# Another hand-written order from the third chunk on, and the rows of maxima loaded one pair a portion

## The chip, the cores and the metric

The kernel runs on one core of a Trainium2 chip. A core has TensorE (PE in the profile; its weight loads are listed as PEld), VectorE (DVE), ScalarE (ACT), GpSimd (POOL) and SyncE (SP, which here only issues DMA transfers). Each engine takes its instructions strictly in the order in which the program lists them, and waits where an operand or a buffer is not ready. The metric is the device time of one execution in microseconds, as the median of several runs.

## The reference

Linear attention over 8 batches, 8 heads, 576 positions and head width 64, then a gated feed-forward over all 4608 tokens:

```python
q_s = softmax(q, over the head width);  k_s = softmax(k, over the positions)
kv  = einsum('bhsd,bhse->bhde', k_s, v)
x   = einsum('bhsd,bhde->bhse', q_s, kv)      # -> 4608 tokens x 512
a, b = x @ w_a, x @ w_b                       # 512 x 1536 each
out = (a * b) @ w_out                         # 1536 x 512
```

All in float32. The kernel gets its precision by splitting an operand into a high and a low part (tiles xo, ws, gh/gl, qhl) and adding three products: high by high, high by low, low by high.

## The kernel before

**Chunks, pairs, portions.** The 4608 tokens are worked on in nine chunks (0 to 8) of 512. Chunk 0 runs beside the loading and conversion of the weights. From chunk 1 on a chunk is six *pairs* of feed-forward blocks (loop at L1392). One pair makes seven products instead of eight (a Strassen-Winograd step on 2 x 2 blocks): A11 into kx, S2 into ky, S3 into ka, S1 into kp, A12 onto kx, S4 onto kp, A22 onto ka (L1434 to L1471). Each is twelve matmuls with 256 columns. kx, ky, ka and kp are banks of PSUM, and there are few: ky and kp share one, and a second product into kx, kp or ka may start only when DVE or ACT has read the first (L1437, L1455, L1441), as the next pair's first product may only when the last has been read (L1457, L1468, L1473). Beside the seven products a pair holds the output projections of the pair before (`run_pending`, matmuls into po with 512 columns, L867), and three calls of `attend` (L1425, L1450, L1465).

**Attention of the next chunk.** While chunk c is multiplied, the attention for chunk c + 1 is computed in *portions*, one at each call of `attend` (class Spread), 15 in a chunk. `attention_tasks` builds the list of portions. For a chunk from the fourth (index 3) on it holds: portions 0 to 4, the maxima and sums of q's softmax (L675 to L683), which are transposed on PE (pst, L689), copied (sst, L691) and written to DRAM as dq (L693); portions 0 to 5, the keys of the next batch: loads (L503, L509), the maximum over the positions (L524 to L526 on DVE, L515 on POOL), exponential (L547, L550), and the product with v (pk, L585); then the *rows*: for each of four head pairs g, dq's rows of maxima and of sums are loaded back and spread over 64 partitions each (`q_rows`, four transfers "mr<-dq", L719), together with a transposed block of q ("qtt<-in_q_late", L707); at last, for each g, the row of maxima is added to that block (L725), ACT takes the exponential (L726), the result is split (L343, L346), multiplied with kv (px, L764) and scaled by the row of sums (xf, L963). For chunks 4 to 8 the row loads of group g stood in portion 6 + g and its use in portion 10 + g and 11 + g; for chunk 3 two groups share a portion.

**Weights.** From chunk 2 on the seven weight operands of a pair come from DRAM, 512 KB each ("ws<-dw", L478), into eight buffers; those of a chunk's last pair are held for the next chunk's first. All loads and stores are issued on SP's queue. A load waits there until the product eight operands before it has been made, and everything behind it on the queue waits too.

**The order.** The text `ORDER` (L28) lists for each engine the instructions of the first chunks one by one. An item is `name:place*count`: of the instructions traced under that name and not yet listed, take the one at this place (0 if not written), count times. `pair.k`, `proj.k`, `attend.k`, `early.k`, `late.k` and `wj.k` are the products and their DVE and ACT work, the projections, the portions, the operands made from x for the next chunk, and the load of weight operand j, of pair k, counted from chunk 1's first; so pair.6 to pair.11 are chunk 2. `arrange` (L1305) chains the instructions of an engine in that order. What the list does not name comes behind it, in the order that the compiler's planner finds by simulating the program: from what is ready, first what was traced first. Before, the list ends on PE within pair.10, on SP with a weight load for pair.11; chunks 3 to 8 are the planner's.

Of the kernel before, what the change touches and what calls it, by code (L numbers as in the profile page):

```python
# [213 lines left out]
    ),  # L214
    "Pool": (
# [4 lines left out]
    ),  # L220
# [37 lines left out]
def linear_attention_then_gated_ffn(  # L258
# [18 lines left out]
    nc = tc.nc  # L277
# [15 lines left out]
    NI = w_ab.shape[0]  # L293
# [97 lines left out]
    def load_f(f):  # L391
# [7 lines left out]
        with tc.issue_after(ins.ins):  # L399
            nc.sync.dma_start(out=raw, in_=w_out[f])  # L400
# [520 lines left out]
    def attention_tasks(c):  # L921
# [48 lines left out]
        for i in range(max(len(stats), len(steps))):  # L970
            seq.append((stats[i] if i < len(stats) else []) + (steps[i] if i < len(steps) else []))
# [560 lines left out]
```

## Time and profile before

| | us |
|---|---|
| median of 3 runs | 945.16 (944.64 to 946.18) |
| the profiled execution | 942.09 |
| its span, first to last instruction | 940.3 |
| mean granted clock of TensorE | 0.998 |

A row of the timeline gives the start and the duration in us, the engine, the line, the operation, the tile written and those read, and the count of like instructions merged into the row; the bracket at its end gives the idle time of that engine just before, and what ended it. SPq is SP's queue. In a row of the windows the columns are the stretch, its length, the busy time and count of PE, PEld, DVE, ACT and POOL, the granted clock of TensorE (1.00 is full speed), the mean busy share of the DMA engines and GB/s. Matmuls overlap and their ends are modelled, so waits of PE are best seen from start to start.

### The profile page before, as it was taken

The numbers are of one execution on the slowest core, as the hardware profiler recorded it, in microseconds if no ns is written. First come the engines' busy times: TensorE is split into PE (matmuls) and PEld (weight loads), VectorE is DVE, ScalarE is ACT, GpSimd is POOL, SyncE is SP. The second block draws the span as 40 slices with busy tenths as digits, with TensorE's granted clock in tenths as the row PEclk, the third lists the DMA queues.
The fourth block names the chain that finished last, engine by engine and source line by source line (L and its number), as shares of the span: only waits on it lengthen the run. The fifth ranks groups of instructions, "written<-read, shape, count | busy, mean of one in ns | idle before, by whom it ended". The sixth has DMA issues, their size and how long they took to land.

```text
span 940.3 us, 17539 instructions
## 1 busy us (share of the span) xinstructions
PE 925.3 (98%) x6565; PEld 837.1 (89%) x6565; DVE 615.2 (65%) x1218; ACT 394.2 (42%) x1094; POOL 107.8 (11%) x88
## 2 busy tenths in 40 slices
PE   8999999999999999999999999999999999999998
PEld 6777789999889899999999999999999998999997
DVE  7998898778655677467656574666657454744433
ACT  8988775435522245133613271324424351322111
POOL 2555434420000000000100010000000000000000
PEclk9999999999999999999999999999999999999999
DMA  9989899989779879983999288945996388637761
GB/s 355 362 293 374 326 327 337 325 295 309 261 252 293 260 262 352 336 281 111 345 268 353 90 302 280 374 167 188 331 343 226 102 292 304 204 108 263 252 218 51
DMA packets 88947, 253.27 MB, mean 269 GB/s; under 512 B 10720, under 2 KB 11296, under 8 KB 88864
## 3 DMA queue, kind: packets, MB, share of 16 engines
q1 hardware_dynamic: 88864, 252.16, 76.5%
q8 instruction: 52, 0.85, 0.4%
q14 instruction: 31, 0.25, 0.1%
HBM read 213.09 MB, written 36.93 MB: 266 GB/s over the span
## 4 chain that ended last, share of the span: by engine, by line
PE 93%; DMA 2%; DVE 2%; SPq 1%; ACT 1%; issue 0%; POOL 0%; DVEq 0%
PE po L867 30%; PE ka L838 14%; PE kp L838 14%; PE kx L838 14%; PE pt L808 7%; PE ky L838 7%; PE px L764 2%; PE pk L585 2%; DMA ws<-dw 2%; PE po L853 1%; SPq L719 1%; PE px L752 1%; DMA kt_first<-in_kt 0%; DVE mc L1122 0%; PE pq L739 0%
## 5 line engine op out<-in xcount | busy, mean ns | idle before, releaser
L867 PE MATMUL po<-wo_w,gh 128*128 128x512 f32 x840 | 264.4, 396 | 0.0
L838 PE MATMUL ka<-xo,ws 128*128 128x256 f32 x1152 | 181.5, 283 | 2.7 <-DVE u L1441 1.9
L838 PE MATMUL kx<-xo,ws 128*128 128x256 f32 x1152 | 183.9, 282 | 0.0
L838 PE MATMUL kp<-xo,ws 128*128 128x256 f32 x1152 | 176.0, 283 | 0.0
L867 PEld LDWEIGHTS po<-wo_w,gh 128*128 128x128 f32 x840 | 151.6, 189 | 25.3 <-issue 0.4
L838 PEld LDWEIGHTS ka<-xo,ws 128*128 128x128 f32 x1152 | 160.1, 190 | 8.8 <-issue 3.2
L838 PEld LDWEIGHTS kx<-xo,ws 128*128 128x128 f32 x1152 | 160.5, 189 | 4.9
L838 PEld LDWEIGHTS kp<-xo,ws 128*128 128x128 f32 x1152 | 156.9, 189 | 5.3 <-DVE cc L1455 0.2
L867 PE MATMUL po<-wo_w,gl 128*128 128x512 f32 x420 | 153.7, 396 | 0.0
L343 ACT CAST gh<-cc 128x512 fp32r<-128x512 f32 x96 | 58.0, 620 | 146.8 <-DVE cc L1469 131.8
L1456 ACT COPY cc<-kx 128x256 f32<-128x256 f32 x48 | 17.9, 372 | 179.9 <-PE kx L838 174.9
L867 PEld LDWEIGHTS po<-wo_w,gl 128*128 128x128 f32 x420 | 78.1, 188 | 15.2 <-DVE gl L346 0.4
L838 PE MATMUL ky<-xo,ws 128*128 128x256 f32 x576 | 86.8, 281 | 2.2 <-DMA ws<-dw 1.1
L1468 DVE TENSOR_TENSOR cc<-kp,u 128x512 f32<-128x512 f32 x48 | 33.1, 690 | 85.1 <-PE kp L838 84.7
L808 PE MATMUL pt<-xo,ws 128*128 128x512 f32 x288 | 87.1, 418 | 0.0
L678 ACT ACTIVATE qt<-qt,st 128x64 f32<-128x64 f32 x224 | 75.4, 340 | 18.4 <-DVE st L675 15.6
L838 PEld LDWEIGHTS ky<-xo,ws 128*128 128x128 f32 x576 | 76.9, 189 | 3.9 <-DVE qtt L725 1.3
L346 DVE TENSOR_TENSOR gl<-cc,gh 128x512 fp32r<-128x512 f32 x96 | 67.0, 706 | 15.0 <-ACT gh L343 12.3
L1455 DVE TENSOR_TENSOR cc<-kp,u 128x512 f32<-128x512 f32 x48 | 33.1, 691 | 66.6 <-PE kp L838 66.2
L808 PEld LDWEIGHTS pt<-xo,ws 128*128 128x128 f32 x288 | 53.0, 188 | 17.4 <-issue 4.3
L515 POOL PARTITION_ALL_REDUCE mx<-m x20 | 17.7, 895 | 438.8 <-DVE m L526 419.1
L1437 ACT COPY u<-kx 128x512 f32<-128x512 f32 x48 | 28.0, 583 | 63.1 <-PE kx L838 55.6
(150 smaller groups left out, 1116.9 us busy)
## 6 DMA issues: line engine op xcount, KB each, us to landing
ws<-dw SPq DMA_DIRECT2D x260, 512.0 KB, 5.5
dw<-ws SPq DMA_DIRECT2D x42, 512.0 KB, 6.4
mr<-dq SPq DMA_DIRECT2D x112, 128.0 KB, 4.5
raw<-in_w_ab SPq DMA_DIRECT2D x24, 512.0 KB, 7.2
out<-ot SPq DMA_DIRECT2D x36, 256.0 KB, 5.0
vt<-in_v SPq DMA_DIRECT2D x28, 325.0 KB, 6.8
qt<-in_q SPq DMA_DIRECT2D x32, 256.0 KB, 5.2
kt<-in_k SPq DMA_DIRECT2D x24, 320.0 KB, 4.9
```

The costliest lines, as they stand in the source:

```text
L343: nc.scalar.copy(out=hi, in_=src)
L346: return nc.vector.tensor_tensor(out=lo, in0=src, in1=hi.bitcast(F32), op=ALU.subtract)
L585: nc.tensor.matmul(pk[h * D:(h + 1) * D], kt[:, j, h], vt[:, j, h], start=(j == 0), stop=(j == J - 1),)
L678: nc.scalar.activation(out=qt[:, j, h], in_=qt[:, j, h], func=AF.Exp, bias=st[:, h, 0, j:j + 1], accum_out=st[:, h, 1, j:j + 1],)
L764: nc.tensor.matmul(px[:, s], w, m[:, s], start=(i == 0), stop=(i == 2))
L808: nc.tensor.matmul(pt, w[:, wp], x[g][:, xp], start=(g == 0 and i == 0), stop=(g == NP - 1 and i == 2),)
L838: ins = nc.tensor.matmul(pt[:, n], w[:, n, wp, c], x[:, xp, c], start=(first and n == 0 and i == 0), stop=(i == 5), skip_group_check=True,)
L867: ins = nc.tensor.matmul(po[t], a[:, ts], wo[f][:, w], start=(f == ends[0] and i == 0), stop=(f == ends[1] and i == 2),)
L1437: nc.scalar.copy(out=u2, in_=kx)
L1455: nc.vector.tensor_tensor(out=cc[:, 3], in0=kp, in1=u3, op=ALU.add)
L1456: nc.scalar.copy(out=cc[:, 0, 0], in_=kx[:, 0])
L1468: nc.vector.tensor_tensor(out=cc[:, 1], in0=kp, in1=u2, op=ALU.add)
```

## The change

Three edits. The kernel's arithmetic, its tiles and its transfers stay the same in kind and number.

1. In `ORDER`, the lists of all five engines are replaced from a point in chunk 2's first pair on (on PE, from the entry after "pair.6:23*3 proj.6 proj.6:1"). Up to that point they stay as they were. The new PE list ends seven matmuls into pair.11, the one of SP with w5.11, the first load of chunk 4's attention and the first store of chunk 1.
2. `load_f` drops the `issue_after` that put the load of w_out behind that of w_ab. SP's list, which names these loads one by one, is unchanged there.
3. `attention_tasks`, for chunks 4 to 8: portions 6 and 7 are left empty; the rows of group g and its block of q are in portion 8 + g; their use stays in portions 10 to 14.

The diff, with most of the list left out:

```diff
     "PE": (
...
-        "pair.6 proj.6:2 pair.6:24 proj.6:7 pair.6 proj.6:3 pair.6:23*3 proj.6 proj.6:1 pair.6*4 "
...
-        "attend.10*3 pair.10 attend.10 "
+        "pair.6 proj.6:2 pair.6:24 proj.6:7 pair.6 proj.6:3 pair.6:23*3 proj.6 proj.6:1 pair.6*8 "
...
+        "attend.10 pair.11*5 pair.10 attend.10 pair.11 attend.10 pair.11 "
     "DVE": (
...
-        "early.5 pair.5 attend.6 attend.6:3 late.5 attend.6:1 attend.6:2 late.5 pair.6 pair.6:1 "
-        "attend.6:2 pair.6 attend.6:2 attend.7:3 attend.7 attend.6:1 pair.6:1 pair.6*2 pair.6:1*2 "
-        "pair.7 attend.6:1 attend.6:2*3 pair.6*2 attend.7:5 pair.7 attend.7:5 pair.7 attend.6 "
-        "pair.7:1 attend.6:1 attend.7:7 attend.7 attend.7:6*2 attend.7:1 attend.7*2 attend.7:1 "
-        "attend.6*2 pair.7 attend.7:2 attend.7:1 attend.6 attend.7 pair.7*2 pair.7:1 pair.7 "
...
-        "pair.9:1 pair.9*2 attend.9 attend.9:1 pair.9 attend.9 pair.10*2 early.11 attend.9 pair.10 "
-        "attend.9*2 pair.10:1 pair.10*2 "
+        "early.5 attend.6 attend.6:3 attend.6:1 pair.5 attend.6:1 pair.6 late.5*2 pair.6 attend.6:4 "
+        "attend.6:1*2 pair.6 attend.6:1 attend.7:3 attend.6 pair.6:1 pair.6 attend.7 pair.6 "
+        "pair.6:1*2 attend.7:5 pair.6 pair.7 attend.6*5 pair.6 pair.7 attend.7:5*2 attend.7:6*2 "
+        "attend.7:2 pair.7 pair.7:1 attend.7*2 attend.6 attend.7 pair.7 attend.7:2 attend.7:1*2 "
+        "attend.7 pair.7:3 attend.6 pair.7*3 attend.7 pair.7 attend.7*3 pair.8*2 attend.7 attend.8 "
...
+        "pair.9 attend.9 pair.9:1 pair.9*6 attend.9 pair.10 attend.7 pair.10 attend.9:1 attend.9 "
+        "pair.9 pair.10 attend.9 pair.10 attend.9:1 attend.9 pair.10:1*2 early.11:1 pair.10 "
     "Activation": (
...
-        "attend.6:4 attend.6:3 attend.6 pair.6 late.5 attend.6:1 attend.7 attend.6 attend.7:5 "
-        "attend.7:7 proj.6:1 attend.7:7 attend.7:6 attend.7:2 proj.6:2 attend.7:6 attend.7:2 pair.7 "
-        "attend.7:7 pair.6 attend.7:6 attend.7:5 proj.6 attend.7 attend.7:2 proj.6 pair.6 attend.7:2 "
-        "pair.7 attend.7*2 attend.7:1 attend.7 pair.7 pair.8 pair.7 attend.8*2 pair.8*2 attend.9 "
...
+        "attend.6:4 attend.6:3 attend.6 late.5 pair.6 attend.6 proj.6:1 attend.6 proj.6:2 attend.7:6 "
+        "pair.6 proj.6*2 pair.7 attend.7:11 attend.7:3 attend.7:10 attend.7:11 attend.7:7 attend.7:6 "
+        "attend.7:5 pair.6 attend.7:3 attend.7:1 attend.7 attend.7:1 pair.7 attend.7:2 attend.7:1*2 "
+        "attend.7*2 pair.8 attend.7 pair.7*2 attend.8 pair.8 attend.8 pair.8 pair.9 attend.9*2 pair.8 "
...
     "Pool": (
...
-        "sums.0*8 sums.1*4 sums.2*4 sums.4 sums.3*2 sums.4 sums.3*2 sums.4*2 attend.6:1 attend.6 "
-        "attend.7*2 "
+        "sums.0*8 sums.1*4 sums.2*4 sums.4 sums.3*2 sums.4 sums.3*2 sums.4*2 attend.6*2 attend.7:1 "
+        "attend.7 "
     "SP": (
...
-        "attend.7 attend.6:2 w2.7 w1.7 proj.0 attend.6*2 w4.7 w3.7 w5.7 attend.7 w6.7 attend.7:1 w0.8 "
-        "attend.7*2 w2.8 w1.8 w4.8 attend.7 w3.8 w6.8 attend.8:8 w5.8 attend.8 attend.8:1 w0.9 w1.9 "
...
+        "attend.7 attend.6:2 attend.6 w1.7 attend.6 w2.7 proj.0 w4.7 attend.7 w3.7 w0.8 attend.7:1 "
+        "w6.7 w5.7 w2.8 attend.7:1 attend.7 w1.8 attend.8:8 w4.8 attend.7 attend.8:8 w3.8 w6.8 "
...
+        "attend.8 w3.11 attend.8 w6.11 w5.11 attend.12 proj.6 "
...
@@ load_f
-        with tc.issue_after(ins.ins):
-            nc.sync.dma_start(out=raw, in_=w_out[f])
+        nc.sync.dma_start(out=raw, in_=w_out[f])
...
@@ attention_tasks
+        last = pipeline(last)
+        if c > 3:
+            begin = 3 * NI - 3 - len(last) - 2
+            seq += [[] for _ in range(len(seq), begin)]
+            for g in range(NP):
+                seq[begin + g:begin + g + 1] = [rows[g:g + 1] + turned[g:g + 1]]
+            for n, now in enumerate(last):
+                seq[begin + n + 2:begin + n + 3] = [(seq[begin + n + 2] if n + 2 < NP else []) + now]
+            return seq
         if roomy(c):
 
             step = 2 if c < 4 else 1
             seq += [rows[g:g + step] + turned[g:g + step] for g in range(0, NP, step)]
-        return seq + pipeline(last)
+        return seq + last
```

`pipeline` staggers the steps of the four groups, so that `last` has five entries for four groups; with NI = 6 that makes begin = 8.

77 rows, old and new, of the table ORDER are left out of this document.

## The prediction

> **What bounds the kernel now.** I read the page first, then the timeline of PE, then the windows (for the granted clock), then the timelines of the engines that PE waited for.
>
> ```profile
> span 940.3 us, 17539 instructions
> ...
> PE 925.3 (98%) x6565; PEld 837.1 (89%) x6565; DVE 615.2 (65%) x1218; ACT 394.2 (42%) x1094; POOL 107.8 (11%) x88
> ...
> PE 93%; DMA 2%; DVE 2%; SPq 1%; ACT 1%; issue 0%; POOL 0%; DVEq 0%
> ```
>
> TensorE holds 93% of the chain that ended last, and the change neither adds nor removes a matmul. So the time can only move by what PE waits and by the clock it gets. The timeline of PE, from the first changed entry of its list (counted along the trace, that is at 239.2 us) to the end, has these starts after an idle time; the bracket gives it and what ended it:
>
> ```profile
> 242.77 0.28 PE L838 MATMUL kp<-xo,ws 128*128 128x256 f32 x1
> 244.98 0.36 PE L838 MATMUL ka<-xo,ws 128*128 128x256 f32 x1 [1.93 <-DVE u L1441]
> ...
> 266.76 0.27 PE L689 MATMUL pst<-ident,st 128*64 128x128 f32 x1 [0.90 <-DVE st L683]
> ...
> 270.47 0.45 PE L585 MATMUL pk<-vt,kt 128*64 128x65 f32 x7 [0.84 <-ACT kt L550]
> ...
> 322.29 0.33 PE L764 MATMUL px<-qhl,kvh 128*128 128x192 f32 x1 [1.19 <-DVE xf L963]
> ...
> 491.50 0.48 PE L838 MATMUL ka<-xo,ws 128*128 128x256 f32 x2 [0.77 <-DMA ws<-dw]
> ...
> 588.75 0.99 PE L838 MATMUL kx<-xo,ws 128*128 128x256 f32 x7
> 590.81 0.35 PE L838 MATMUL ky<-xo,ws 128*128 128x256 f32 x1 [1.07 <-DVE gl L346]
> ...
> 789.05 0.60 PE L838 MATMUL ky<-xo,ws 128*128 128x256 f32 x3 [1.12 <-DMA ws<-dw]
> ```
>
> They add up to 7.82 us. Between them matmuls follow each other evenly: seven in 0.99 us, so (0.99 - 0.28) / 6 = 0.12 us each for 256 columns. The first wait costs more than itself, as the windows show (the column after POOL is the granted clock):
>
> ```profile
> 246.50:247.00 0.50, 0.50 (x4) 0.50 (x4) 0.50 (x1) 0.00 (x0) 0.44 (x1) 0.50 1.03 406
> 247.00:249.00 2.00, 2.00 (x10) 1.90 (x10) 2.00 (x4) 1.15 (x3) 0.00 (x0) 0.50 0.85 284
> ...
> 246.00:250.00 4.00, 4.00 (x19) 3.64 (x18) 3.23 (x5) 1.91 (x5) 0.94 (x2) 0.57 0.86 311
> 320.00:324.00 4.00, 2.81 (x23) 2.60 (x22) 3.05 (x6) 0.78 (x2) 0.00 (x0) 1.00 0.56 185
> ```
>
> From 246 to 250 us the clock was 0.57, which costs 4 x 0.43 = 1.7 us; around the 1.19 us wait at 322 it stayed 1.00. So 7.82 + 1.7 = 9.5 us is all there is to gain, 1% of the time.
>
> **The change, part by part.** *The joined list, chunk 2 (239 to about 325 us).* The list fixes each engine's order there, so I followed what each waiting matmul needs through the old rows and the new order.
>
> Wait at 245. The second product into ka (L1471) overwrites the sums that L1441 reads, and L1441 was late on DVE:
>
> ```profile
> 242.62 0.37 ACT L1456 COPY cc<-kx 128x256 f32<-128x256 f32 x1 [3.77 <-PE kx L838]
> 242.89 0.62 ACT L343 CAST xo<-xt 128x512 fp32r<-128x512 f32 x1
> ...
> 238.53 0.68 DVE L1438 TENSOR_TENSOR u<-ky,u 128x512 f32<-128x512 f32 x1
> ...
> 243.54 0.69 DVE L346 TENSOR_TENSOR xo<-xt,xo 128x512 fp32r<-128x512 f32 x1 [1.72 <-ACT xo L343]
> 244.15 0.68 DVE L1441 TENSOR_TENSOR u<-ka,u 128x512 f32<-128x512 f32 x1
> ...
> 245.08 0.28 DVE L526 TENSOR_TENSOR m<-m,kt 128x128 f32<-128x128 f32 x1
> ...
> 246.26 1.05 DVE L547 TENSOR_TENSOR kt<-kt,mx 128x640 f32<-128x640 f32 x1
> ```
>
> DVE stood 1.72 us for the cast of `late.5`, which ACT held behind the copy of kx. The new lists put that cast before the copy ("late.5 pair.6" for "pair.6 late.5") and L1441 before the two late differences ("pair.6 late.5*2"). What is late next: ahead of L1441 the list now has the first L547, which needs GpSimd's reduction. L1438 starts at 238.53; then one 128x512 difference, the small L682, L524 and L526 bring L526 to about 240.1; from L526 to L547 it was 246.26 - 245.08 = 1.18, so L547 at 241.3, L1441 about 1.0 later, at 242.3, and PE goes on 244.98 - 244.15 = 0.83 after that, 243.1. PE comes to this matmul as the 26th entry instead of the 28th, at about 242.7: 0.4 us are left, and 0.1 where L1455, now behind the two differences, frees kp. A wait so short should not lower the clock. Gain 1.93 + 1.7 - 0.5 = **3.1** (bounds 0 and 3.6).
>
> Waits at 267 and 270:
>
> ```profile
> 263.94 0.28 PE L838 MATMUL kx<-xo,ws 128*128 128x256 f32 x1
> ...
> 264.26 0.38 ACT L1456 COPY cc<-kx 128x256 f32<-128x256 f32 x1 [5.18 <-PE kx L838]
> ...
> 264.87 0.34 ACT L678 ACTIVATE qt<-qt,st 128x64 f32<-128x64 f32 x1
> ...
> 265.33 0.17 DVE L682 TENSOR_SCALAR st<-st 128x8 f32<-128x8 f32 x1 [1.43 <-ACT qt L678]
> ...
> 266.67 1.39 POOL L515 PARTITION_ALL_REDUCE mx<-m  x2 [19.73 <-DVE st L683]
> ...
> 268.09 1.56 DVE L547 TENSOR_TENSOR kt<-kt,mx 128x640 f32<-128x640 f32 x2 [0.99 <-POOL mx L515]
> ```
>
> Here two of the exponentials stood behind pair.7's copy of kx; from the last kx matmul to L682 it took 1.39 us. In the new list it is three, and L682 of the last group (`attend.7`, fifth) stands on DVE **before** L1455 of pair.7, on which the next product into kp waits: 1.39 + 0.34 + 0.08 + 0.69 + 0.15 = 2.65 us after the last kx matmul. The list gives PE eight 256-column entries (0.12) and four 512-column ones (0.23) to do meanwhile, 1.88: a new wait of 0.8. Then POOL's two reductions come in the reverse order ("attend.7:1 attend.7"), so the first L547 on DVE waits for both (L526 to L547 then 1.8 us, from the rows), and L1473, which frees ka for pair.8, stands behind both L547: some 8.1 us after the last kx matmul, where PE comes at 7.2: another 0.9. Removed 1.74, added 1.7: **0** (bounds -1.5 and 1.7).
>
> Wait at 322:
>
> ```profile
> 320.85 0.69 DVE L346 TENSOR_TENSOR qhl<-qtt,qhl 128x512 fp32r<-128x512 f32 x1 [2.38 <-ACT qhl L343]
> 321.46 0.68 DVE L963 TENSOR_TENSOR xf<-px,mr 128x512 f32<-128x512 f32 x1
> ...
> 301.42 0.37 ACT L1456 COPY cc<-kx 128x256 f32<-128x256 f32 x1 [8.27 <-PE kx L838]
> ...
> 301.82 0.42 DVE L1457 TENSOR_TENSOR cc<-kx,cc 128x256 f32<-128x256 f32 x1 [0.94 <-ACT cc L1456]
> ```
>
> L963 frees the one bank of px, but stood behind a difference that waited 2.38 us for ACT. The new list has L963 first ("attend.9:1 attend.9"): gain **1.1** (bounds 0 and 1.2). In return the first kx matmul of pair.9 and pair.10 comes 0.9 and 0.8 us after the last of the pair before, while copy and product of kx need about 0.32 + 0.40 + 0.42 + 0.15 = 1.3: two new waits, **-0.8** (bounds -2 and 0).
>
> *The rows of maxima, attention of chunks 4 to 8.* SP's timeline in chunk 5, and the landing time of a weight load:
>
> ```profile
> 570.06 0.47 SPq L693 DMA_DIRECT2D dq<-sst  x1
> 571.05 1.10 SPq L478 DMA_DIRECT2D ws<-dw  x2
> 573.47 7.48 SPq L719 DMA_DIRECT2D mr<-dq  x12
> ...
> 582.23 2.37 SPq L719 DMA_DIRECT2D mr<-dq  x4
> ...
> 585.33 3.56 SPq L478 DMA_DIRECT2D ws<-dw  x6
> ...
> ws<-dw SPq DMA_DIRECT2D x260, 512.0 KB, 5.5
> ```
>
> Sixteen row transfers leave in one run and hold SP for 12 us; the next weights leave at 585.33 and, 5.5 later, land at 590.8, where PE's wait ends (the view names gl, but the wait ends with that landing). The waits at 491 and 789 are the same. The change makes no transfer more or fewer. It moves two of a chunk's four groups behind weights in the traced order: group 0 to portion 8, 1 to 9 (both still ahead of these weights), 2 to 10, 3 to 11. So eight transfers of 7.48 / 12 = 0.62 go before the weights, which leave at about 578.5 and land by 584, while PE asks for them at 590.81 - 1.07 = 589.7. A group is used two portions (11 us) after its new place, so no one waits for it. Gain 0.77 + 1.07 + 1.12 = **3.0** (bounds 0 and 3.0; no loss: with the other eight rows (5 us) behind the second of these weights, the third still leaves at about 582.5, earlier than now).
>
> *Load order of raw weights* (the dropped issue_after): SP's list still writes that order out. Zero; without that cover one weight load at the start would trade places with its neighbour.
>
> Sum: 3.1 + 0 + 1.1 - 0.8 + 3.0 = 6.4 us. The profiled execution took 942.09 us (span 940.3 and 1.8 around it), so it would take 935.7; the median of the three timed runs is 945.16, which gives **938.8**.
>
> **The rivals.**
> *The run of rows stays* (20%). Beyond the list the planner orders SP, and it takes what is ready: all sixteen rows are ready when dq has landed, their buffers being free. If the weights' buffers come free in its reckoning just after, all sixteen go first again. For it: vt loads are issued far ahead of need; against it, the planner kept the rows in traced order. Gain 6.4 - 3.0 = 3.4: 941.8.
> *More goes than I see* (10%): the waits I put into pairs 7 to 10 are covered: gain 9: 936.
> *The slow stretch stays* (5%): the 0.50 clock has another cause than the wait. One wait of seven shows it, the longest, and it follows 1.3 us behind, so I think it unlikely. 938.8 + 1.7 = 940.5. The Trainium skill ("TensorE: Matmul & The Clock Gate", Why this matters for your kernels) has the clock fall only after idle gaps of about 3 us; by that rule 1.93 us would not do it. The trace disagrees as far as it goes: half clock after 1.93 us.
> *The list only moves its waits* (8%): 4 us of new ones in pairs 6 to 10 and the rows half mended: gain about 1.5: 943.7, within 0.2%.
> *Slower* (7%): DVE is blocked in pair.7 by the second key load. L524 of that tile stands ahead of L1455; the new SP list has that load behind w3.7 and w0.8, which wait for a weight buffer. If it lands 5 us after DVE gets there, PE waits about 5 at pair.7's second kp product and the clock halves again (1.7); with new waits of 2 behind it and the rows not mended, 4.2 - 8.7 gives 4.5 us of loss: 949.7. With the rows not mended it decides from a wait of about 2.5 us on (4.2 - 2.5 - 1.7 - 2 = -2.0).
>
> **How the numbers follow.** Forecast 50%, 938.8; rivals 20, 10, 5, 8 and 7%. 0.2% (1.9 us) is about what a measurement can tell from no change here. Faster: 50 + 20 + 10 + 5 = 85%, of which I leave 1 for a tie: 84; same 9, slower 7. The range takes in the run of rows and the full gain, with 0.8 beyond for the spread of the runs shown (944.64 to 946.18): 935.2 to 942.9.
>
> **What would show it.** Right: no PE wait over 0.6 us at pair.6's second ka product and clock 1.00 behind it; waits of 0.8 and 0.9 in pair.7 and at pair.8's first ka; none at the last px of chunk 3; on SP at most eight mr in a run, and weights between. Wrong: sixteen mr in one run in chunks 4 to 7; a wait of 2 us or more followed by 0.50; or waits on mr or on dq at L725.

## The result and the profile after

| kernel | runs | median us | lowest to highest |
|---|---|---|---|
| before | 4 | 945.67 | 944.64 to 946.79 |
| after | 4 | 937.25 | 935.81 to 937.30 |

The ratio is 0.9907, with a 95% interval of 0.989 to 0.9924: the change takes off 8.4 us. The prediction was 938.8 us, with a range of 935.2 to 942.9. The profiled execution of after took 935.81 us against 942.09 before, 6.3 less, where the sum had said 6.4. That agreement is better than the prediction deserves: its parts were off in opposite directions, as the experiments show.

The page of after, its head and the first line of the chain:

```profile
span 934.0 us, 17535 instructions
...
PE 924.7 (99%) x6565; PEld 835.2 (89%) x6565; DVE 618.0 (66%) x1218; ACT 394.0 (42%) x1094; POOL 107.9 (12%) x88
...
PE 95%; DVE 2%; DMA 1%; ACT 0%; POOL 0%; issue 0%; SPq 0%; DVEq 0%; POOLq 0%
```

TensorE's busy time is that of before within 0.6 us (925.3 to 924.7), while the span is 6.3 us shorter. So what went is waiting. The timeline of PE in after has these idle times left in the stretch of the joined list (start, duration, line, and in the bracket the idle time and what ended it; after.py's lines stand some three above before.py's):

```profile
243.48 0.36 PE L835 MATMUL ka<-xo,ws 128*128 128x256 f32 x1 [0.38 <-DVE u L1447]
...
262.80 0.39 PE L835 MATMUL kp<-xo,ws 128*128 128x256 f32 x1 [0.51 <-DVE cc L1461]
...
268.28 0.38 PE L835 MATMUL ka<-xo,ws 128*128 128x256 f32 x1 [0.33 <-DVE cc L1479]
...
283.31 0.36 PE L761 MATMUL px<-qhl,kvh 128*128 128x192 f32 x1 [0.28 <-ACT qhl L341]
...
298.52 0.38 PE L835 MATMUL kx<-xo,ws 128*128 128x256 f32 x1 [0.23 <-DVE cc L1463]
```

Four of the five stand where the prediction put a wait (it named none at the px product), and they add up to 1.73 us. Before, the four in this stretch were 1.93, 0.90, 0.84 and 1.19. The windows show the rest: no idle PE and full clock (the column 1.00) behind the first wait, at the old place of the last px, and where the weights were late:

```profile
245.00:247.00 2.00, 2.00 (x18) 1.96 (x17) 1.55 (x6) 1.46 (x3) 0.70 (x1) 1.00 0.99 332
...
320.00:324.00 4.00, 4.00 (x33) 3.96 (x33) 3.39 (x7) 2.45 (x5) 0.00 (x0) 1.00 0.95 278
...
490.00:500.00 10.00, 10.00 (x64) 8.78 (x63) 5.04 (x9) 2.88 (x5) 0.00 (x0) 1.00 1.02 350
588.00:596.00 8.00, 8.00 (x52) 7.26 (x52) 5.18 (x9) 2.03 (x4) 0.00 (x0) 1.00 1.04 332
788.00:796.00 8.00, 8.00 (x52) 7.22 (x52) 4.13 (x7) 2.17 (x4) 0.00 (x0) 1.00 1.02 417
```

SP's timeline in chunk 5 (start, time to issue, line, count) shows what was done to the rows of maxima:

```profile
566.63 0.47 SPq L690 DMA_DIRECT2D dq<-sst  x1
567.62 0.93 SPq L475 DMA_DIRECT2D ws<-dw  x2
569.10 4.93 SPq L716 DMA_DIRECT2D mr<-dq  x8
574.12 1.00 SPq L475 DMA_DIRECT2D ws<-dw  x2
575.18 3.38 SPq L716 DMA_DIRECT2D mr<-dq  x4
...
583.27 2.37 SPq L716 DMA_DIRECT2D mr<-dq  x4
```

Eight rows, two weights, four rows, more weights, four rows: the first weights behind rows leave 7.5 us after dq instead of 15.3 (585.33 - 570.06 before).

### The profile page after: what moved, and what is told of

Same layout as the page of the kernel before. It is cut to its first block, busy times and chain, and to the rows that moved or that the text cites. A ratio compares the mean times of both kernels' runs of the same rounds, so it can differ in the third digit from the quotient of the medians.

```text
span 934.0 us, 17535 instructions
## 1 busy us (share of the span) xinstructions
PE 924.7 (99%) x6565; PEld 835.2 (89%) x6565; DVE 618.0 (66%) x1218; ACT 394.0 (42%) x1094; POOL 107.9 (12%) x88
## 4 chain that ended last, share of the span: by engine, by line
PE 95%; DVE 2%; DMA 1%; ACT 0%; POOL 0%; issue 0%; SPq 0%; DVEq 0%; POOLq 0%
PE po L864 31%; PE kx L835 14%; PE kp L835 14%; PE ka L835 14%; PE pt L805 7%; PE ky L835 7%; PE px L761 2%; PE pk L582 2%; PE po L850 1%; PE px L749 1%; DMA kt_first<-in_kt 1%; DVE xo L344 0%; POOL mx L512 0%; DVE kt L544 0%; DVE mc L1128 0%
## 5 line engine op out<-in xcount | busy, mean ns | idle before, releaser
L835 PE MATMUL ka<-xo,ws 128*128 128x256 f32 x1152 | 177.7, 282 | 0.7 <-DVE u L1447 0.4
L835 PEld LDWEIGHTS ka<-xo,ws 128*128 128x128 f32 x1152 | 157.9, 189 | 6.7 <-issue 0.6
L1461 DVE TENSOR_TENSOR cc<-kp,u 128x512 f32<-128x512 f32 x48 | 33.2, 691 | 62.7 <-PE kp L835 62.2
```

Of the source, the lines that this page charges most:

```text
L835: ins = nc.tensor.matmul(pt[:, n], w[:, n, wp, c], x[:, xp, c], start=(first and n == 0 and i == 0), stop=(i == 5), skip_group_check=True,)
L1461: nc.vector.tensor_tensor(out=cc[:, 3], in0=kp, in1=u3, op=ALU.add)
```

## The experiments

Twelve experiments ran in four groups (e0, one more profiled execution of before, is not in the table). Each group ran on a chip of its own beside fresh runs of before, whose median was 942.80, 944.62, 944.86 and 943.34 us. Compare a kernel with the before of its own group.

| kernel | median us | before | lowest to highest | ratio (95%) |
|---|---|---|---|---|
| e1 rows only | 938.19 | 942.80 | 937.66 to 939.81 | 0.9958 (0.9943 to 0.9973) |
| e2 list only | 943.97 | 942.80 | 940.19 to 947.49 | 1.0005 (0.9981 to 1.0028) |
| e3 before, one cast first | 942.90 | 942.80 | 940.39 to 948.78 | 1.0009 (0.9987 to 1.0031) |
| e5 after, again | 936.39 | 944.62 | 935.82 to 937.12 | 0.9929 (0.9908 to 0.9949) |
| e6 rows only, again | 937.88 | 944.62 | 937.29 to 938.85 | 0.9945 (0.9924 to 0.9966) |
| w1 after, waits out | 933.63 | 944.62 | 932.27 to 934.88 | 0.9899 (0.9878 to 0.9921) |
| e4 rows on GpSimd's queue | 945.09 | 944.62 | 941.34 to 947.04 | 1.0005 (0.9986 to 1.0023) |
| e7 rows in half as many transfers | 940.03 | 944.86 | 937.67 to 941.69 | 0.9939 (0.9917 to 0.9960) |
| e8 rows of a quarter's width | 940.57 | 944.86 | 938.30 to 943.66 | 0.9962 (0.9941 to 0.9984) |
| e9 rows and one cast first | 936.93 | 944.86 | 935.98 to 938.83 | 0.9914 (0.9886 to 0.9941) |
| e10 after, rows in one run | 938.15 | 943.34 | 936.57 to 940.20 | 0.9946 (0.9925 to 0.9968) |

The runs of before beside them spread by 6 to 10 us in each group, while the four runs of the result had spread by 2. That spread was the first surprise. Most of it goes with the unbroken run of rows, and the granted clock has a share in it, as the experiments show.

### The two halves of the change, each alone (e1, e2), and before once more (e0)

e1 keeps before's list and takes the code hunk of the change; e2 takes the list and keeps before's code:

```diff
 # e1: ORDER of before, and in the attention's sequence
+        if c > 3:
+            begin = 3 * NI - 3 - len(last) - 2
...
 # e2: ORDER of after, the sequence of before
+        "pair.6:15 pair.6:3 proj.6 pair.6:3*2 ...
```

> Before with the change of the portions alone (rows of group g in portion 8 + g for chunks 4 to 8), the list and the load order as before. My theory (the sixteen row transfers in one run on SP hold back the next weights): PE's waits at 491, 591 and 789 us go, the waits at 245 to 322 us stay, 3 us less than before (ratio 0.9965 to 0.997), at most eight mr in a run on SP. Rival (the planner puts all sixteen behind dq again, and the gain is the list's): same time as before within 0.5 us.

> After with the portions as before: the new list alone. My theory: waits at 491, 591 and 789 are there again (0.8 to 1.2 us each), the first part up to 325 us as in the changed kernel; 3.4 us less than before, and with the rows' 3 us the whole of the change. Rival (something beyond the waits that I counted, since the medians differ by 8.4 and the two profiles by 6.3): the list alone gives 5 us or more.

> The kernel before once more, for a second profile of it. If PE's waits and the slow stretch of clock are the program's own, they stand at the same places within 0.1 us (1.93 at 245, clock 0.57 from 246 to 250, 0.77 at 491, 1.07 at 591, 1.12 at 789). If the 2 us by which the difference of the medians (8.4) passes that of the profiles (6.3) lie in waits that come in some executions only, a further wait or slow stretch shows here that the first profile did not have.

The rows alone take off 4.6 us and bring the spread down to 2.2; e1's profile has the four waits of the list and none on a weight. The list alone takes off nothing that can be seen. Its profiled execution, the slowest of its twelve, has in its own stretch the waits of after (0.50 at most), but behind the row runs in chunks 3 and 4 the timeline of PE has

```profile
390.65 1.80 PE L836 MATMUL ky<-xo,ws 128*128 128x256 f32 x12 [1.77 <-DMA ws<-dw]
...
496.30 1.68 PE L836 MATMUL ka<-xo,ws 128*128 128x256 f32 x12 [3.43 <-DMA ws<-dw]
```

both on weights, and both with a clock of 0.50 behind them (the windows 392 to 394 and 498 to 500). In the execution that the prediction was read from, the first of these did not exist and the second was 0.77. The second execution of before (e0, 948.1 us) had yet other sizes there, 1.17 and 2.13, while its four waits in the listed stretch had the same 1.93, 0.90, 0.84 and 1.19 as in the first. So the listed waits are the program's own, and those behind the row run depend on when transfers land in that execution. e2's interval reaches from 1.8 us below before to 2.6 above, so the 3.4 us that were expected are missed. Whether a smaller gain of the list is lost in this tail, or only hidden by its spread, the runs do not show.

### One exchange of the list (e3, e9)

```diff
 "Activation", chunk 2
-... attend.6:4 attend.6:3 attend.6 pair.6 late.5 ...
+... attend.6:4 attend.6:3 attend.6 late.5 pair.6 ...
```

> Before with one exchange in ScalarE's list: the cast of late.5 ahead of pair.6's copy of kx. My theory: DVE no longer waits 1.72 us, L1441 comes at about 242.4, PE's wait at 245 shrinks from 1.93 to 0.3 us, and with it goes the stretch of clock 0.50 behind it: 3.3 us less than before. Rival (the slow stretch has another cause): the stretch of 0.50 stays, 1.6 us less. Rival (DVE's two late differences still hold L1441): under 1 us less.

e3 made this exchange alone in before and missed by its median: 942.90 against 942.80, with an interval from 1.2 us below to 2.9 above. In its tail it waited for weights as e2 did (0.97 at 391 us, 1.91 at 493). Its profile still showed the wait at pair.6's second ka product gone and the clock there at 1.00. e9 is the same exchange with the rows of the change, so that no late weight disturbs behind it:

> The rows of the change, and of the joined list only the one exchange on ScalarE: the cast of late.5 ahead of pair.6's copy of kx. With the tail clear, its worth stands alone: the wait at pair.6's second ka product falls from 2.09 to about 0.3 us, so 1.8 us below the rows alone (937.88), 936.1, which is what the whole joined list brings (936.39). Rival: freed there, the time is lost at the next places (266 and 270 us, 1.06 and 1.0 now): within 0.5 of the rows alone.

936.93, 0.9 us less than the rows alone in the group before, and 7.9 below its own before, against 6.7 for the rows alone. The timeline of PE of e9 has the product without any bracket, with L1465's copy and the cast exchanged and nothing else:

```profile
245.54 0.36 PE L838 MATMUL ka<-xo,ws 128*128 128x256 f32 x1
```

The waits at 266, 269 and 321 us stayed as they were (0.90, 0.84 and 1.19), so the rival that the time comes back at the next places fell.

The medians come from two groups of runs. The traces give a closer measure: the time between the same two matmuls, counted along PE's timeline. From the 1511th matmul, about where the lists begin to differ, to the 6561st, 5 us before the end, the rows alone (e6) take 690.76 us and e9 688.95: 1.81 less, what was expected. That e9's profiled execution is only 0.4 us shorter in all comes from its start: it reaches the 1511th matmul 1.43 us later than e6, behind a clock of 0.57 from 11 to 15 us that e6 doesn't have. The prediction's account of this wait holds: DVE stood for a cast that ScalarE kept behind a copy.

### What the joined list is worth with the tail clear (e5, e6)

Both ran without an edit of their own: e5 is after, e6 is e1.

> The changed kernel once more, unaltered, beside the rows alone on the same chip. Both theories: 937.0 (936 to 938) and a spread of its runs of about 1.5 us, since no wait on a late weight load is left. Theory A (the joined list is worth what its waits are worth, 3.4 us by the prediction, up to 5 where the clock had dropped behind the wait at pair.6's second ka product): 1.2 to 3 us below the rows alone. Theory B (the list is worth nothing, as it seemed when it ran alone before a disturbed tail: 943.97 against 942.8): within 0.5 us of the rows alone. The first look at the rows alone (938.19, span 936.2) against this kernel's (span 934.0) leans to A.

> The rows of the change with the list of before, again. The tail has no waits in it, so the list's own waits stand alone: 938.5 (937.5 to 940). Theory A: a wait of 2.1 at pair.6's second ka product, 1.1 and 1.0 at the two places of pair 7 and 8, 1.35 at the last px of chunk 3, 5.5 in all against some 3.0 of the changed list, so 2 to 2.5 us above the changed kernel, 3.7 to 4.2 where the clock halves behind the first wait. Theory B: no more than 0.5 above.

936.39 against 937.88, 1.5 us, and the two sets of runs do not overlap. Theory A named 1.2 to 3 in the one text and 2 to 2.5 in the other; theory B fell. The profiles differ as much (spans of 934.4 and 935.7). The waits do not: 4.86 us of brackets in e6 against about 1.7 in e5, 3.1 us. So the new list loses some 1.8 us in what no bracket shows (3.1 - 1.3).

The count of matmuls says where. It divides the trace at the 2301st, in chunk 3, behind all that the lists name:

| us between matmuls | 1511th to 2301st | 2301st to 6561st |
|---|---|---|
| before (the two profiles) | 111.80, 111.78 | 584.53, 587.27 |
| after | 108.89 | 580.90 |
| e6 rows only | 110.24 | 580.51 |
| e5 after, again | 108.92 | 580.58 |
| e9 rows and one cast first | 108.44 | 580.51 |
| e2 list only | 108.87 | 591.28 |

The 111.8 of before holds the slow clock behind the first wait. The loss of the 1.8 us is inside the listed stretch: the tails of e5, e6 and e9 agree within 0.1 us. Take the steps from one matmul's start to the next there, and compare each with the median of its kind. Steps that are over 0.15 us too long add up to 5.50 us in e6 and 2.96 in e5, 2.5 less. The shorter delays add up to 2.1 and 3.3, 1.2 more, in many small pieces; why the new order has more of these isn't shown. So the list is worth 1.3 us here, less than the 1.8 of the one exchange of e9.

The first wait has the same size in e6 as in before, but here no slow stretch follows. The timeline of PE and the windows of e6:

```profile
245.93 0.36 PE L838 MATMUL ka<-xo,ws 128*128 128x256 f32 x1 [1.93 <-DVE u L1450]
```

```profile
246.00:248.00 2.00, 2.00 (x15) 1.83 (x16) 1.75 (x4) 0.00 (x0) 1.43 (x2) 1.00 0.99 387
248.00:250.00 2.00, 2.00 (x16) 1.86 (x15) 2.00 (x4) 1.19 (x3) 0.00 (x0) 1.00 0.86 279
```

### What holds the weights back (e4, e7, e8, e10)

The prediction said that the run of sixteen rows holds SP for 12 us, so that weights leave late. Theory C kept that; theory D said that the rows fill the DMA engines, whoever issues them. e4 lets GpSimd issue the rows of chunks 4 to 8, e7 halves their number at the same bytes, e8 quarters the bytes at the same number:

```diff
 # e4
-                nc.sync.dma_start(
+                (nc.gpsimd if c > 3 else nc.sync).dma_start(
 # e7, c > 3: two transfers a group, 128 partitions each
+            for w in range(2):
+                nc.sync.dma_start(out=rows[w], in_=dq[g, 0, w].unsqueeze(0).broadcast_to([P, T]))
...
 # e8, c > 3: s = T // 4, the rest zeroed by GpSimd
-                    out=rows[w][h * D:(h + 1) * D], in_=dq[g, h, w]...
+                    out=rows[w][h * D:(h + 1) * D, :s], in_=dq[g, h, w][:s]...
```

> The kernel before with the row loads of chunks 4 to 8 issued by GpSimd's queue instead of SP's; the sixteen may leave in one run as before, but SP is free for the weights. Theory C (what delays the weights is the time that SP needs to issue sixteen row loads, 0.62 us each): the weights leave right after dq's, land in time, and the waits at 390, 491, 590 and 790 us are gone: 938.5 as with the rows alone, spread about 1.5 us. Theory D (the sixteen loads fill the DMA engines, whoever issues them, so that weights that leave beside them land late): the waits stay, with weight landing times well above 6 us beside the run: 941 to 944 and a spread of several us.

> The kernel before, with the rows of chunks 4 to 8 loaded by half as many transfers of twice the size: eight of 256 KB a chunk instead of sixteen of 128 KB (both halves of the partitions get the first head's row, so the second head's maxima and sums are left out). SP's share of a run falls from about 12 us towards 6; the bytes that the DMA engines move are the same. Theory C (SP's issuing holds the weights back): the weights leave some 5 us earlier, as in the changed kernel, the waits at 390 to 400, 491 to 500, 590 and 790 us are gone: 938 to 940, spread under 2 us. Theory D (the bytes hold the DMA engines): nothing gained, 943 to 945 and a spread of several us.

> The kernel before, with the row loads of chunks 4 to 8 as many as before but of a quarter of the width (128 of 512 columns; the rest of each row is set to zero by GpSimd, so three quarters of the rows are left out). SP issues as many transfers, some 10 to 12 us a run; the DMA engines move a quarter of the bytes. Theory C (SP's issuing): 943 to 945 and a spread of several us, as before. Theory D (the bytes): the waits behind the run are gone, the four of the list stay: 938 to 940, spread under 2 us. If the packets' number counts and not their bytes, as many packets of 512 B take nearly as long and the result is as under C, but then e7 gains nothing either.

e4 gained nothing, with SP free. The view of DMA issues between 478 and 488 us (count, size, median us from issue to landing) shows why; before first, then e4:

```profile
ws<-dw SPq DMA_DIRECT2D x3, 512.0 KB, 6.0
mr<-dq SPq DMA_DIRECT2D x9, 128.0 KB, 4.7
```

```profile
ws<-dw SPq DMA_DIRECT2D x4, 512.0 KB, 16.2
mr<-dq POOLq DMA_DIRECT2D x9, 128.0 KB, 9.7
```

The first weight that stood behind the run leaves 5.2 us after dq's store (at 478.61) instead of 16.0, and the four of this stretch take 16.2 us to land instead of 6.0. PE waits for them as before:

```profile
391.30 1.66 PE L838 MATMUL ka<-xo,ws 128*128 128x256 f32 x12 [0.52 <-DMA ws<-dw]
397.52 0.59 PE L838 MATMUL kx<-xo,ws 128*128 128x256 f32 x3 [1.76 <-DMA ws<-dw]
```

So SP's time alone was not the answer. The Trainium skill ("DMA: Bandwidth & Descriptors", Issuing engines are not separate DMA queues) has transfers of all issuing engines run on the same 16 DMA engines, and another issuer save only the issuing time; e4 agrees, with 16.2 us. Whether GpSimd's way of issuing adds to that figure wasn't tried: the view lists its rows under a queue of another kind (q0, software_dynamic) than SP's (q1, hardware_dynamic).

But e8 is no clean case for theory D either. Its rows are light: the DMA share (the column after the clock) falls in the run, windows of before and then of e8:

```profile
478.00:482.00 4.00, 4.00 (x30) 3.73 (x29) 0.69 (x1) 0.00 (x0) 0.00 (x0) 1.00 0.89 221
```

```profile
478.00:482.00 4.00, 4.00 (x28) 3.60 (x27) 0.13 (x2) 0.00 (x0) 0.00 (x0) 1.00 0.20 55
```

SP still issues them one by one, and the weights leave hardly sooner, 15.5 us after dq instead of 16.0. SP's timeline of before and then of e8, and PE's of e8 in chunk 3:

```profile
470.08 0.47 SPq L693 DMA_DIRECT2D dq<-sst  x1
...
472.77 9.15 SPq L719 DMA_DIRECT2D mr<-dq  x12
...
482.87 2.51 SPq L719 DMA_DIRECT2D mr<-dq  x4
...
486.11 2.30 SPq L478 DMA_DIRECT2D ws<-dw  x4
```

```profile
470.71 0.47 SPq L693 DMA_DIRECT2D dq<-sst  x1
...
473.41 8.69 SPq L723 DMA_DIRECT2D mr<-dq  x12
...
483.15 2.36 SPq L723 DMA_DIRECT2D mr<-dq  x4
...
486.24 1.81 SPq L478 DMA_DIRECT2D ws<-dw  x4
```

```profile
392.11 1.67 PE L842 MATMUL ka<-xo,ws 128*128 128x256 f32 x12 [0.67 <-DMA ws<-dw]
```

One wait of 0.67 is left in this execution, the second fastest of its twelve, and by the medians 4.3 us are gained. e7 does the opposite, fewer issues and the same bytes, and gains 4.8: its eight rows hold SP for 4.7 us instead of 11.7, and weights leave at 483.33, 10.3 us after dq.

```profile
473.04 0.47 SPq L693 DMA_DIRECT2D dq<-sst  x1
...
476.68 3.75 SPq L719 DMA_DIRECT2D mr<-dq  x6
...
481.29 0.97 SPq L719 DMA_DIRECT2D mr<-dq  x2
...
483.33 1.02 SPq L478 DMA_DIRECT2D ws<-dw  x2
```

e7's profiled execution is the slowest of its ten, and yet PE waits for no weight in it: its tail from the 2301st matmul takes 580.77 us, that of e6 580.51. Its rows were no lighter on the DMA engines than those of e0 and e3 (a packet of 2 KB on SP's queue took 84 ns, the median in the runs of chunks 3 and 4 of all three), and e0 and e3 do wait for weights behind them. So fewer issues took the lateness away in this execution, with the same bytes, as theory C had it.

Both spread more than the rows of the change do (4.0 us in e7 and 5.4 in e8, against 1.6 for e6). In e7 that is mostly the clock: its four fastest runs, 937.67 to 938.48 us, have a mean granted clock of 0.999, and its three slowest, 940.30 to 941.69, have 0.995 and 0.996. In e8 the slow runs weren't profiled.

So neither theory stands alone. A weight's lateness is its issue behind the run plus its landing behind the run's bytes; less of either brings most of the gain, and moving time from the one to the other (e4) brings none.

e10 asks whether the place of the rows in the traced order matters or only the break between them. It is after with all four pairs traced in one portion:

```diff
-                seq[begin + g:begin + g + 1] = [rows[g:g + 1] + turned[g:g + 1]]
+                seq[begin + g:begin + g + 1] = [(rows if g == 1 else []) + turned[g:g + 1]]
```

> The changed kernel, but all four pairs of rows of a chunk are traced in one portion (the ninth) instead of one in each of four; the planner then again sends the sixteen in one run as soon as dq has landed, ahead of the weights that the changed kernel sends between them. Theory R (the unbroken run is what cost the time: a weight that leaves behind it lands late): waits on ws come back at 390 to 400, 491 to 500 and 590 us, 1 to 3 us each in some of these places, 940 to 944, and the spread of the runs is several us again. Rival (the place in the order of the trace is what counts, later than before): no wait on ws, 936.4 (935.8 to 937.3).

The planner again sent sixteen in one run, and the result lies between the two expectations: 938.15, 5.2 us below before where e5 had 8.2, and a spread of 3.6 us against 1.3. SP's timeline in chunk 5:

```profile
567.30 0.47 SPq L690 DMA_DIRECT2D dq<-sst  x1
...
569.79 10.36 SPq L716 DMA_DIRECT2D mr<-dq  x16
580.26 0.99 SPq L475 DMA_DIRECT2D ws<-dw  x2
```

The weights leave 13.0 us after dq, between the 7.5 of after and the 15.3 of before. Its profiled execution was the fastest of its seven runs and shows no late weight, so the waits of the others weren't seen. By the medians, the unbroken run gives back about 3 us of the rows' gain; neither theory names that size.

### A version that beats both (w1)

w1 is after with the entries moved that the remaining waits name. What moved, in words (line numbers of after; the text below calls attend.8's entries attend.9):

```
 DVE   L544 of attend.6's first tile:  behind pair.6's L1461, not ahead of L1447
 DVE   attend.7, L679 (fifth):         behind pair.7's L1461 and L1464
 DVE   attend.7, L523 (second tile):   ahead of pair.7's L1461
 DVE   attend.8, first L344 of qhl:    ahead of pair.8's L1461
 ACT   attend.8, first L341 of qhl:    ahead of pair.8's copy of kx
 POOL  attend.7's two reductions:      in the order in which they are used
 PE    first kx products of pair.9, pair.10: a few matmuls later
```

> The changed kernel with eight entries of its joined list moved: L544 of the first tile of attend.6 behind L1461 of pair.6; L679, L523 of attend.7 out of L1461's way in pair.7 and the key maximum ahead of it; GpSimd's two last reductions in the order in which they are used; the last cast and difference of qhl of attend.9 one place earlier; the first kx products of pair.9 and pair.10 a few matmuls later. If the waits that the prediction named cost what they show (0.54, 0.68, 0.49, 0.45, 0.39 and 0.4 in small ones), and nothing new takes their place: 1.5 to 2.3 us below the changed kernel, 935.0. Rival: each move only makes the next producer late (DVE has no slack there): within 0.5 us of it, with the same sum of waits at other instructions.

933.63 us against 936.39, and the two sets of runs don't overlap: 2.8 us below after, 11.0 below before. Head and chain of its page, and the one idle time that PE's timeline has left from 239 to 330 us:

```profile
span 932.4 us, 17538 instructions
...
PE 98%; DVE 1%; DMA 1%; issue 0%; ACT 0%; SPq 0%; POOL 0%; DVEq 0%; POOLq 0%
```

```profile
257.37 0.36 PE L835 MATMUL kp<-xo,ws 128*128 128x256 f32 x1 [0.38 <-DMA ws<-dw]
```

Between the 1511th and the 6561st matmul w1 takes 687.08 us and e5 689.50, 2.4 less. The rival, that DVE has no slack and each move only makes another producer late, fell.

## Why the prediction was right, and where not

**The bound.** TensorE's work is the bound and only its waits can go. That held: busy time moved by 0.6 us, the span by 6.3.

**The wait at 245.** The chain was right. The timeline of DVE of after:

```profile
241.90 0.83 DVE L544 TENSOR_TENSOR kt<-kt,mx 128x640 f32<-128x640 f32 x1 [0.62 <-POOL mx L512]
242.65 0.68 DVE L1447 TENSOR_TENSOR u<-ka,u 128x512 f32<-128x512 f32 x1
```

L544 was put at 241.3 and came at 241.90, L1447 at 242.3 and came at 242.65; PE was to wait 0.4 and waits 0.38. e9 shows the cause alone. What was wrong is the term of 1.7 us for the clock, entered as certain. The same 1.93 us wait stood in seven profiled executions (both of before, e1, e4, e6, e7 and e8), and the clock fell behind it in three: both of before, and e7. Where it fell it cost 1.5 us: from the 1511th to the 1601st matmul those three take 14.2 us, the other four 12.7. Over executions the term is worth 3/7 of that, by estimate 0.65 us.

**The waits at 267 and 270.** Predicted at nothing gained: 1.74 removed, 0.8 and 0.9 added. The two new waits came at the named instructions, L1461 of pair.7 behind the small L679, and L1479 behind both L544, but of 0.51 and 0.33. The timeline of DVE of after, for the first:

```profile
261.98 0.17 DVE L679 TENSOR_SCALAR st<-st 128x8 f32<-128x8 f32 x1 [2.50 <-ACT qt L675]
262.06 0.68 DVE L1461 TENSOR_TENSOR cc<-kp,u 128x512 f32<-128x512 f32 x1
```

The mechanism was right and the sizes were too large by 0.9 in sum.

**The wait at 322** went, as predicted. Of the waits set against it, that at the first kx of pair.10 came, at 0.23; that of pair.9 did not, and instead a px product waits 0.28 for the cast of qhl.

**The list in all.** Predicted at 3.4 us, measured at 1.5 by the medians (e5 against e6) and 1.3 by the count of matmuls. Without the clock's 1.7, which neither of the two profiles shows, the sum would have said 1.7. That this is so near the measured value is luck: the brackets fell by 3.1 us and not by 1.7, and delays that no bracket shows, and that weren't foreseen, took the difference back.

**The rows.** The order on SP came as written: eight rows, then weights. The size was 3.0 us, read from one execution; measured are 4.6 (e1) and 6.7 (e6). The failed step is that size: it took the waits of 0.77, 1.07 and 1.12 for the program's, where they are one draw of something that reached 3.43 elsewhere. The execution on the page of before was a favourable draw: its 942.09 us lay 3 us below the median of the runs shown with it, and the longer waits of the other runs were in the medians, not in the sum. The step's reason, that the sixteen transfers "hold SP for 12 us", is half of it, as e4, e7 and e8 show.

**The sum.** 3.4 + 3.0 against 1.5 and 4.6 to 6.7. The list was priced too high and the rows too low. On the two profiled executions the table above gives 2.9 for the list, where the clock fell before, and 3.6 for the rows, so the two errors cancel: that the sum came to 6.4 against 6.3 is luck. In the medians the rows win, and the change brought 8.4.

**The rivals.** None came whole. "More goes than I see" came in part: of the 2.5 us of new waits put into pairs 7 to 10, 1.35 came (0.51, 0.33, 0.28 and 0.23), and 937.25 lies about midway between that rival's 936 and the forecast. The run of sixteen rows did not stay in after; e10 shows what it costs when it does. No key load blocked DVE in pair.7. That the slow stretch would stay with another cause did not happen, but its reason was better than the 5% it got: the wait does not settle the clock by itself.

## What to carry to other kernels

Take two or three profiled executions of a kernel before pricing its waits: in this kernel those that stayed the same to 0.03 us came from the program's own order, those that changed were transfers that landed late, and only the first kind could be read off one page. The slow clock behind a wait belongs to the second kind. To price a new order, compare the time between the same two matmuls in two traces; the sum of the idle times said 3.1 us where 1.3 were gained. A long run of small transfers ahead of weights cost twice here, in the issuer's time and in the DMA engines', so break it with the weights that are needed next rather than hand it to another issuer. Where an order is written out by hand, one exchange that frees an engine from a cast may be worth as much as the whole rewrite. Find it first, and move further entries only for the waits that are then left.

## What the runs showed of the hardware

**The same wait, with and without the slow clock.** The timeline of PE and the windows of e7, beside those of e6 above:

```profile
248.12 0.52 PE L842 MATMUL ka<-xo,ws 128*128 128x256 f32 x1 [1.93 <-DVE u L1445]
```

```profile
248.00:250.00 2.00, 1.88 (x9) 1.91 (x10) 1.40 (x4) 0.00 (x0) 1.36 (x2) 0.54 1.01 397
250.00:252.00 2.00, 2.00 (x11) 1.81 (x11) 2.00 (x4) 0.94 (x2) 0.07 (x1) 0.61 1.04 374
```

The wait is 1.93 us in both, and the clock is 0.54 behind it in e7 and 1.00 in e6. From 239 to 930 us it fell behind all five waits for weights of 1.76 us or more (1.76 in e4, 1.77 and 3.43 in e2, 1.91 in e3, 2.13 in e0), and never behind one of 1.58 (e4) or less. In the first 20 us it fell in three executions (0.57 from 16 to 20 us in e0 and e7, from 11 to 15 in e9), where the longest waits shortly before it were 1.59, 1.59 and 1.29; in e6 one of 1.49 stood there without a fall. The Trainium skill ("TensorE: Matmul & The Clock Gate", What's actually happening) has the clock fall after at least one idle window of about 3.4 us, in a window that runs freely, so that the same kernel shows different counts of slow matmuls from run to run. The chance agrees with these runs; the length does not, since 1.93 us were enough three times in seven.

**Spread that goes with the order on one queue.** Runs of before beside each other reach from 939.21 to 947.71 us on one chip (17 runs); the same list with the rows broken up, from 937.29 to 938.85 (6 runs). The two programs differ in the order of transfers alone. A part of the spread is the clock: of the 21 runs of before beside e7, the six with a granted clock of 1.000 took 939.46 to 944.09 us, the eleven with 0.995 or 0.996 took 942.16 to 949.56. How much of that is the clock's own and how much the waits in front of it, the runs that weren't profiled don't say.
